# One PSUM tile of eight banks, priorities as a virtual time, an earlier load and a split last output, in a fused attention and expert kernel

## The chip, the cores and the metric

The kernel runs on one core of a Trainium2 chip. The metric is the device time of one execution in microseconds (us). TensorE (PE) multiplies matrices into PSUM, ScalarE (ACT) and VectorE (DVE) read PSUM and work on SBUF, GpSimd (POOL) works on SBUF and issues the loads, SyncE (SP) issues the stores.

## The reference

Four batches of block attention with eight heads, 768 positions and 64 channels are followed by a top-1 mixture of eight experts. A Sinkhorn iteration (five times exp, row norm, column norm) turns a small 8x8 matrix of each head into `P`, which mixes the eight blocks of keys and of values; each query block then attends to its own mixed block.

```python
for _ in range(5):
    P = np.exp(P - np.max(P, axis=-1, keepdims=True))
    P = P / (np.sum(P, axis=-1, keepdims=True) + 1e-09)
    P = P / (np.sum(P, axis=-2, keepdims=True) + 1e-09)
k_sorted = np.einsum('bhij,bhjcd->bhicd', P, k_b)
v_sorted = np.einsum('bhij,bhjcd->bhicd', P, v_b)
attn = softmax(scale * q_b @ k_sb^T)
x = (attn @ v_sb).transpose(0, 2, 1, 3).reshape(B * S, H * D)
expert_idx = np.argmax(x @ w_gate, axis=1)
out[mask] = gate_w[mask, None] * (np.maximum(xe @ w1[e], 0.0) @ w2[e])
```

## The kernel before

The four batches run as four attentions and four experts. The kernel guesses the expert of a batch from a vote over its values, loads that expert's two weight matrices alone, applies it to all 768 rows, and does rows that chose another expert only behind a branch. Work is written as tasks; a planner in Python (`Plan`) gives each task an engine, a start and PSUM banks from costs in a table, and `emit` writes the instructions in the order of those starts. Nothing is reordered later: every engine runs its instructions in that order and waits on semaphores.

The tasks of batch b, with the lines at which their instructions stand in the profile:

- loads of q, v and k (L322, L339), and of the weights w1 and w2 (L347, L350), all issued from POOL; `chain` at the end of the kernel fixes their order on POOL's queue. The weights wait for the vote.
- "vote sum", "vote pick" (PE, L547 and L556) and "vote read" (DVE, L563 and L564): the guess of the expert, which POOL reads (L570) before it issues the weight loads.
- "relay" (L586): a copy that turns v_in into vr. "q" (PE, L601), "k" (L622) and "v" (L649), each with copies out of PSUM on ACT (L307) or DVE (L309). k and v multiply with pk and pv, which are made from `P`; `P` comes from the Sinkhorn chain on ACT (L454) and DVE (L458, L460, L461).
- for each of eight steps i: scores "s" (PE, L679), "exp" (ACT, L688), values "a" (PE, L695), normalization "n" (DVE, L705 and L706), transpose "t" (PE, L714), copy "x" (L307 or L309).
- "route" (PE, L739; DVE, L747 and on): the gate weights.
- the expert, twice (two halves of the rows): eight hidden groups "h" (PE, L772) with "relu" (ACT L782 or DVE L784), then three outputs "o", each in two pieces "a" and "b" of four matmuls (PE, L777), weighed by the gate "w" (ACT L788 or DVE L790) and stored (L841).

PSUM is held as four tiles of two banks each:

```python
pairs = [psp.tile([P, 2, 512], F32, tag=f"pair{i}", name=f"pair{i}") for i in range(4)]
PAIRS = (0, 2, 4)            # s, a, later k and v: two banks at once
FFN_BANKS = (4, 5, 6, 7)     # h and o: one bank
```

A task that asks for one bank takes half of a pair tile; the bank comes free when its reader's task ends. A task's priority (`prio`) says who goes first when several could start on an engine: attention b has 10b, its route 10b+6, expert b 10b+15. `emit` also writes matmuls on an idle tile (L83, fillers) where the plan has PE waiting in the first 26 us.

The change and the steps of the prediction touch `Plan.fit`, `Plan.emit` and `Plan.schedule`, the PSUM tiles, `add_attention` (relay, priorities), `add_expert` (the cut of the last output, banks, priorities), and the order of the loads.

Of the kernel before, what the change touches and what calls it, by code (L numbers as in the profile page):

```python
# [35 lines left out]
class Plan:  # L36
# [8 lines left out]
    def __init__(self, dma_at=2.1, dma_us=2.43):  # L45
        self.tasks, self.free = [], {}
        self.bank = [0.0] * 8
        self.dma_free, self.dma_us = dma_at, dma_us
        self.order = []
# [6 lines left out]
    def fit(self, banks):  # L56
        if banks.n == 2:
            spots = [(max(self.bank[i], self.bank[i + 1]), (i, i + 1), 0) for i in range(0, 8, 2)
                     if self.bank[i] is not None and self.bank[i + 1] is not None]
        else:  # L60
            spots = []
            for i in range(8):
                if self.bank[i] is not None:
                    twin = self.bank[i ^ 1]
                    spots.append((self.bank[i], (i,), 0 if twin is None else 1))
        if banks.only is not None:
            spots = [s for s in spots if s[1][0] in banks.only]
        return spots

    def emit(self, nc, idle, pairs, warm, until):  # L70

        held, at = [0.0] * 8, warm
        for t in self.order:
            if t.engine == "pe":
                gap = t.start - at
                while gap > 0.45 and t.start < until:
                    free = [i for i in range(8) if held[i] is not None and held[i] <= at - 0.4]
                    if not free:
                        break
                    i = free[0]  # L80
                    n = min(int(gap / 0.225), 12)
                    for _ in range(n):
                        nc.tensor.matmul(out=pairs[i // 2][:, i % 2, :], lhsT=idle[:, :128],  # L83
                                         rhs=idle, start=True, stop=True)
                    at += n * 0.22
                    held[i] = at
                    gap = t.start - at - 0.2
                at = t.end
            if t.opens is not None:
                for i in t.opens.at:  # L90
                    held[i] = None
            t.run(t.engine)
            if t.closes is not None:
                for i in t.closes.at:
                    held[i] = t.end
# [16 lines left out]
    def schedule(self):  # L112
# [11 lines left out]
        while open_:  # L124
# [49 lines left out]
            if t.lands is not None:  # L174
                if t.lands:
                    self.dma_free = max(self.dma_free, end + 0.9) + t.lands * self.dma_us
                    t.end = self.dma_free + 1.6
                else:
                    t.end = end + 2.3
            if t.opens is not None:  # L180
                spots = [x for x in self.fit(t.opens) if x[0] + 0.12 <= s + 1e-9]
                if t.opens.n == 2:
                    at = min(spots, key=lambda x: (x[0], x[1]))[1]
                else:
                    at = min(spots, key=lambda x: (x[2], x[0], x[1]))[1]
                t.opens.at = at
                for i in at:
                    self.bank[i] = None
            if t.closes is not None:
                for i in t.closes.at:  # L190
                    self.bank[i] = t.end
# [12 lines left out]
def kernel(  # L204
# [19 lines left out]
    P = 128  # L224
# [19 lines left out]
    pairs = [psp.tile([P, 2, 512], F32, tag=f"pair{i}", name=f"pair{i}") for i in range(4)]  # L244

    def bank(banks, j=0):
        i = banks.at[j]
        return pairs[i // 2][:, i % 2, :]

    def both(banks):  # L250
        return pairs[banks.at[0] // 2]
# [284 lines left out]
    PAIRS = (0, 2, 4)  # L536

    def add_attention(b):
        A = 10 * b
# [11 lines left out]
        t1 = add(f"vote sum{b}", {"pe": 0.65}, run_vsum, [v_at[b], m_vm], A - 5, opens=vb)  # L551
        t2 = add(f"vote vm{b}", {"act": 0.2, "dve": 0.2}, lambda e: copy(e, vm, bank(vb)[:, :H]), [t1], A - 5, closes=vb)
# [6 lines left out]
        t3 = add(f"vote pick{b}", {"pe": 0.25}, run_pick, [t2, wv_a, wv_b], A - 5, opens=lb)  # L559
# [6 lines left out]
        t4 = add(f"vote read{b}", {"dve": 0.45}, run_read, [t3], A - 5, closes=lb)  # L566
        val = {}

        def run_w1(e):
# [3 lines left out]
        w1_at[b] = add(f"load w1.{b}", {"pool": 1.3}, run_w1, [t4, *relu_of.get(b - 2, [])], A - 4, lands=2.0)  # L573
        w2_at[b] = add(f"load w2.{b}", {"pool": 0.9}, lambda e: load_w2(val["ev"], i2),
                       outs_of.get(b - 2, []), A - 4, lands=2.0)
        top_at[b] = add(f"top{b}", {"pool": 0.2}, lambda e: nc.gpsimd.tensor_scalar(
            top[b], eids[b][:, 0:1], -1.0, float(E), op0=ALU.mult, op1=ALU.add), [t4], A)
# [4 lines left out]
        for d0 in range(0, D // 2, D // 4):  # L582
            def run_relay(e, d0=d0):
                dst = u32(vr[i2])[:, d0:d0 + D // 4, :HB, 0]
                src = u32(v_in[i2])[:, :, d0:d0 + D // 4]
# [8 lines left out]
        for g in range(3):  # L594
# [9 lines left out]
            t = add(f"q{b}.{g}", {"pe": 0.6}, run_q, [q_at[b][g], mk_ident, *scores_of.get(b - 2, [])], A + 2, opens=qb)  # L604
# [5 lines left out]
            q_ev.append(add(f"q ev{b}.{g}", evac(1024, 1.02, 1.22), run_ev, [t], A + 2, closes=qb))  # L610
# [4 lines left out]
        for g in range(3):  # L615
            kb = Banks(2, PAIRS if b else None)
# [337 lines left out]
```

## Time and profile before

| | us |
|---|---|
| median of 3 runs | 186.6 (184.68 to 187.89) |
| the profiled execution: its time | 185.21 |
| the profiled execution: its span | 183.5 |
| PE busy in the span | 155.2 |
| ACT busy | 95.7 |
| DVE busy | 83.8 |
| POOL busy | 30.3 |

The span runs from the first to the last instruction of the profiled execution; the other 1.7 us lie around it. An engine's busy time counts overlapping instructions once; PE's ends are modelled. The granted clock of TensorE is given in tenths or as a share of 2.4 GHz.

### The profile page before, as it was taken

The numbers are of one execution on the slowest core, as the hardware profiler recorded it, in microseconds if no ns is written. First come the engines' busy times: TensorE is split into PE (matmuls) and PEld (weight loads), VectorE is DVE, ScalarE is ACT, GpSimd is POOL, SyncE is SP. The second block draws the span as 40 slices with busy tenths as digits, with TensorE's granted clock in tenths as the row PEclk, the third lists the DMA queues.
The fourth block names the chain that finished last, engine by engine and source line by source line (L and its number), as shares of the span: only waits on it lengthen the run. The fifth ranks groups of instructions, "written<-read, shape, count | busy, mean of one in ns | idle before, by whom it ended". The sixth has DMA issues, their size and how long they took to land.

```text
span 183.5 us, 5246 instructions
## 1 busy us (share of the span) xinstructions
PE 155.2 (85%) x2271; PEld 96.9 (53%) x2271; DVE 83.8 (46%) x217; ACT 95.7 (52%) x159; POOL 30.3 (17%) x65
## 2 busy tenths in 40 slices
PE   7897988188989789899889799995788999998960
PEld 2365766068655465486565354772554555544520
DVE  5588687347755750087596200572765200500000
ACT  3154975119686444387665264683565454525440
POOL 7993800207500001150000001100000000000000
PEclk9999999957999999999999999999999999999995
DMA  4994599999999991999995116995001303103032
GB/s 42 214 199 69 72 198 194 215 212 153 198 180 230 242 227 32 174 237 231 210 214 142 59 57 98 197 254 91 0 4 57 116 4 114 57 15 148 8 118 64
DMA packets 13770, 24.51 MB, mean 134 GB/s; under 512 B 1328, under 2 KB 6448, under 8 KB 13744
## 3 DMA queue, kind: packets, MB, share of 16 engines
q0 software_dynamic: 9568, 17.83, 55.7%
q1 hardware_dynamic: 4032, 6.19, 9.4%
q8 instruction: 19, 0.31, 0.7%
q10 hardware_dynamic: 144, 0.13, 0.2%
q14 instruction: 7, 0.06, 0.1%
HBM read 35.68 MB, written 6.29 MB: 229 GB/s over the span
## 4 chain that ended last, share of the span: by engine, by line
PE 52%; DMA 18%; ACT 10%; DVE 9%; issue 5%; POOL 1%; POOLq 1%; DVEq 0%; ACTq 0%
PE pair L777 20%; PE pair L772 19%; DMA v_in<-in_v_dram 18%; PE pair L83 4%; ACT o L788 3%; ACT qT L307 3%; PE pair L714 2%; PE pair L649 2%; ACT ksT L307 2%; DVE vr L586 2%; ACT hT L782 2%; PE pair L695 2%; PE pair L679 1%; DVE xT L309 1%; POOL w L350 1%
## 5 line engine op out<-in xcount | busy, mean ns | idle before, releaser
L772 PE MATMUL pair<-xT,w 128*128 128x384 bf16 x256 | 47.2, 329 | 4.4 <-issue 2.1
L777 PE MATMUL pair<-w,hT 128*128 128x512 bf16 x192 | 45.5, 379 | 3.9 <-ACT o L788 2.4
L782 ACT ACTIVATE hT<-pair 128x384 bf16<-128x384 f32 x54 | 24.4, 489 | 27.0 <-PE pair L772 18.7
L772 PEld LDWEIGHTS <-w 128*128 128x128 bf16 x256 | 23.4, 98 | 17.4 <-issue 2.7
L788 ACT ACTIVATE o<-pair,gws 128x512 f32<-128x512 f32 (+1 forms) x23 | 15.4, 677 | 28.1 <-PE pair L777 15.9
L777 PEld LDWEIGHTS <-hT 128*128 128x128 bf16 x192 | 17.8, 97 | 23.1 <-issue 4.9
L688 ACT ACTIVATE ex<-pair 128x768 bf16<-128x768 f32 x32 | 25.0, 815 | 3.3 <-PE pair L679 3.2
L706 DVE TENSOR_TENSOR xo<-pair,rec 96x512 bf16<-96x512 f32 x32 | 22.0, 687 | 1.1
L83 PE MATMUL pair<-idle 128*128 128x512 bf16 x48 | 14.0, 432 | 1.8 <-DVE idle L390 1.3
L714 PE MATMUL pair<-ident,xo 96*128 96x96 bf16 x128 | 10.8, 206 | 5.5 <-DVE xT L309 2.9
L747 DVE TENSOR_REDUCE mx<-pair 128x6 f32<-128x48 f32 x4 | 0.8, 203 | 31.5 <-ACT o L788 31.5
L309 DVE COPY xT<-pair 128x384 bf16<-128x384 bf16 x23 | 8.2, 356 | 14.2 <-PE pair L777 5.4
L714 PEld LDWEIGHTS <-xo 96*128 96x128 bf16 x128 | 7.8, 97 | 11.0 <-issue 5.7
L695 PE MATMUL pair<-vs,ex 128*128 128x65 bf16 x256 | 12.9, 193 | 0.1
L695 PEld LDWEIGHTS <-ex 128*128 128x128 bf16 x256 | 10.7, 97 | 3.8 <-ACT ex L688 1.6
L649 PE MATMUL pair<-pv,vr 128*64 128x64 bf16 x512 | 10.6, 202 | 0.4 <-ACT ksT L307 0.4
L649 PEld LDWEIGHTS <-vr 128*64 128x64 bf16 x512 | 9.8, 118 | 1.3 <-issue 1.3
L679 PE MATMUL pair<-qT,ksT 64*128 64x96 bf16 x256 | 10.1, 205 | 0.4 <-ACT ksT L307 0.2
L790 DVE TENSOR_SCALAR o<-pair,gws 128x512 f32<-128x512 f32 (+1 forms) x2 | 1.2, 617 | 19.2 <-ACT o L788 18.4
L307 ACT COPY qT<-pair 128x1024 bf16<-128x1024 bf16 x9 | 8.8, 1007 | 2.0 <-PE pair L601 1.2
L679 PEld LDWEIGHTS <-ksT 64*128 64x128 bf16 x256 | 6.4, 94 | 5.9 <-issue 3.7
L307 ACT CAST vs<-pair 128x1024 bf16<-128x1024 f32 x9 | 9.2, 1029 | 0.4
(91 smaller groups left out, 150.5 us busy)
## 6 DMA issues: line engine op xcount, KB each, us to landing
w<-in_moe_w_dram POOLq DMA_DIRECT2D x8, 1024.0 KB, 10.7
out_dram<-o SPq DMA_DIRECT2D x23, 256.0 KB, 2.1
q_in<-in_q_dram POOLq DMA_DIRECT2D x4, 768.0 KB, 18.2
v_in<-in_v_dram POOLq DMA_DIRECT2D x4, 768.0 KB, 15.0
k_in<-in_k_dram POOLq DMA_DIRECT2D x3, 768.0 KB, 22.5
k_in<-in_k_dram POOLq DMA_DIRECT2D x3, 256.0 KB, 10.4
out_dram<-o ACTq DMA_DIRECT2D x1, 128.0 KB, 2.3
out_dram<-o SPq DMA_DIRECT2D x1, 128.0 KB, 2.0
```

What stands on the lines that cost most here:

```text
L83: nc.tensor.matmul(out=pairs[i // 2][:, i % 2, :], lhsT=idle[:, :128], rhs=idle, start=True, stop=True)
L307: nc.scalar.copy(dst, src)
L649: nc.tensor.matmul(out=t[f * HP:(f + 1) * HP, u, :], lhsT=vr[i2][:, d // 2, :, d % 2], rhs=pv[b][:, f * H:(f + 1) * H, :].rearrange("p h i ...
L679: nc.tensor.matmul(out=sc[:, r, h4 * BLK:(h4 + 1) * BLK], lhsT=ksT[i2][rows, x].rearrange("p f c -> p (f c)"), rhs=qT[i2][rows, x * CQ:(x ...
L688: te = add(f"exp{b}.{i}", {"act": 0.82}, lambda e, ex=ex, sbk=sbk: nc.scalar.activation(ex[:, :H * BLK].rearrange("p (t c) -> p t c", t=2) ...
L695: nc.tensor.matmul(out=av[:, h // 4, h % 4, :], lhsT=ex[:, h * BLK:h * BLK + P], rhs=vs[i2][:, h * NB + i, :D + 1], start=(h % 4 == 0), st ...
L706: nc.vector.tensor_mul(xo, av[:, :, :, :D], rec.to_broadcast([BLK, 2, 4, D]))
L714: nc.tensor.transpose(out=tp[:, dc, :], in_=xf[:, dc * P:(dc + 1) * P], identity=ident[:BLK, :BLK])
L772: nc.tensor.matmul(out=ps, lhsT=w1t[:, dc, fc * P:(fc + 1) * P], rhs=xT[:, dc, half * NH:(half + 1) * NH], start=(dc == 0), stop=(dc == DC ...
L777: nc.tensor.matmul(out=ps, lhsT=hT[:, fc, s * P:(s + 1) * P], rhs=w2t[:, fc, :], start=(fc == 0), stop=(fc == FC - 1))
L782: nc.scalar.activation(dst, src, ACT.Relu)
L788: nc.scalar.activation(dst, src, ACT.Copy, scale=gw)
```

## The change

The four pair tiles become one tile of eight banks. Of the free banks a single one is still taken beside an occupied one first and among these the one that has been free longest, now of all eight; among equals the highest number goes first. FFN_BANKS becomes None and k, v, s and a lose PAIRS, so every task may take any bank. Priorities become a virtual time: a batch has a span of 100, attention steps are 7 apart from 35 on, an expert's groups spread over the 100 after its attention, so that expert b and attention b+1 carry interleaved numbers. The relay runs on DVE alone, the first batch's in four pieces. The load of v for batch 1 moves ahead of the weights of batch 0. The PE task "swap", on which an ACT copy depends, comes after the first q transposes. `emit` counts fillers with two durations. The last output is computed as two halves of 256 columns in two banks.

```diff
     def fit(self, banks):
...
+        b, got = self.bank, []
+        for i in range(0, 8, banks.n):
+            if banks.only is not None and i not in banks.only:
+                continue
+            if banks.n == 2:
+                if b[i] is not None and b[i + 1] is not None:
+                    got.append((max(b[i], b[i + 1]), 0, i))
+            elif b[i] is not None:
+                got.append((b[i], 0 if b[i ^ 1] is None else 1, i))
+        return got
...
-                while gap > 0.45 and t.start < until:
...
+                while t.start < until and t.start - at > 0.5:
...
+                    us = 0.43 if at < warm else 0.217
+                    nc.tensor.matmul(out=psum[:, free[-1], :], lhsT=idle[:, :128], rhs=idle,
+                                     start=True, stop=True)
...
-    pairs = [psp.tile([P, 2, 512], F32, tag=f"pair{i}", name=f"pair{i}") for i in range(4)]
...
+    psum = psp.tile([P, 8, 512], F32, name="psum")
+
+    def bank(banks):
+        return psum[:, banks.at, :]
 
     def both(banks):
-        return pairs[banks.at[0] // 2]
+        return psum[:, banks.at:banks.at + 2, :]
...
-    PAIRS = (0, 2, 4)
+    SPAN, PREP, STEPS, STEP = 100, 3.5, 35, 7
...
-        for d0 in range(0, D // 2, D // 4):
+        cut = D // 4 if b else D // 8
+        for d0 in range(0, D // 2, cut):
...
-            relays.append(add(f"relay{b}.{d0}", {"dve": 0.47} if b or not d0 else {"pool": 1.2}, run_relay,
-                              [v_at[b], pads["vr", i2], *old], A - 1))
+            relays.append(add(f"relay{b}.{d0}", {"dve": 0.5 if b else 0.27}, run_relay,
+                              [v_at[b], pads["vr", i2], *old], A - 10))
...
-            sbk, ab, tb = Banks(2, PAIRS), Banks(2, PAIRS), Banks(1)
+            sbk, ab, tb = Banks(2), Banks(2), Banks(1)
...
-                     A + 4 + i * 0.1, opens=sbk)
+                     A + STEPS + i * STEP, opens=sbk)
...
-    FFN_BANKS = (4, 5, 6, 7)
+    FFN_BANKS = None
...
-                cuts = ((0, MD // 2, ("act",), "act"), (MD // 2, MD, ("dve",), "sp")) if final else (
-                    (0, MD, ("act", "dve"), "sp"),)
+                cuts = ((0, MD // 2, "act", "act"), (MD // 2, MD, "dve", "sp")) if final else ((0, MD, None, "sp"),)
                 used = []
...
+                for j, (lo, hi_, way, queue) in enumerate(cuts):
+                    pb = Banks(1, FFN_BANKS)
...
         add_attention(b)
         if b == 0:
...
+            swap_t.after.append(q_done[0][0])
...
-    chain += seq
+    seq.remove(v_at[1])
+    chain.append(v_at[1])
+    chain = chain[:5] + [v_at[1]] + seq
...
-    plan.emit(nc, idle, pairs, 2.0, 26.0)
+    plan.emit(nc, idle, psum, 1.3, 5.5, 26.0)
```

What the planner makes of this stands in the built programs. First POOL at the start. Before, from the first pv (a factor for the values of batch 0) on, it reads the vote and issues the weights w1 and w2 of batch 0, and then v, q and k of batch 1:

```order
L518 TENSOR_TENSOR pv_139<-vh,pt_v_138 128x128
L570 TENSOR_LOAD eid_129
L570 ISA x2
L347 ISA
L347 DMA w_0_96<-in_moe_w_dram 128x4x1024
L350 ISA
L350 DMA w_0_98<-in_moe_w_dram 128x8x512
L576 TENSOR_SCALAR top_133<-eid_129 128x1
L339 DMA v_in_73<-in_v_dram 128x3072
L322 DMA q_in_69<-in_q_dram 128x2x1536
L322 DMA k_in_71<-in_k_dram 128x2x1536
```

With the change, from the memsets of vs on:

```order
L386 MEMSET vs_77 48x64 x2
L330 DMA v_in_70<-in_v_dram 128x3072
L384 MEMSET vs_78 128x64
L386 MEMSET vs_78 48x64 x2
L397 IOTA rev_i 128x8
L398 CAST rev<-rev_i 128x8
L374 MEMSET vr_76 128x32x32
L377 MEMSET ksT_74 128x64x16
L436 COPY expand_v<-ident 32x384
L394 MEMSET ones 128x128
L436 COPY expand_k<-ident 32x768
L509 TENSOR_TENSOR pv_136<-vh,pt_v_135 128x128
```

The load of v for batch 1 (L330, v_in_70) has moved from behind the weights to far ahead of the vote, and POOL's copy of v_in into vr is gone from the list.

Second ACT at the start, before (sn is the Sinkhorn matrix, wv the table of the vote, qT the turned queries):

```order
L454 ACT_TABLE_LOAD
L454 ACTIVATE sn_108<-sn_108 32x64 x2
L424 CAST wv_115<-pair0_64 64x4x8 x2
L454 ACTIVATE sn_108<-sn_108 32x64 x2
L307 COPY qT0_74<-pair0_64 128x128x8
L454 ACTIVATE sn_108<-sn_108 32x64
L307 COPY qT0_74<-pair0_64 128x128x8
```

and with the change:

```order
L445 ACT_TABLE_LOAD
L445 ACTIVATE sn_105<-sn_105 32x64 x4
L298 COPY qT0_71<-psum_64 128x128x8
L415 CAST wv_112<-psum_64 64x4x8 x2
L445 ACTIVATE sn_105<-sn_105 32x64
L298 COPY qT0_71<-psum_64 128x128x8 x2
```

The two wv casts have moved from behind the second exponential to behind the fourth and the first qT copy.

Third ACT where expert 1 and attention 2 run together, before (hT is a relu, ex an exponential, o a weighed output):

```order
L307 CAST vs0_80<-pair2_66 128x64x16
L782 ACTIVATE hT2_102<-pair3_67 128x384
L307 CAST vs0_80<-pair0_64 128x64x16
L688 ACTIVATE ex0_82<-pair1_65 128x768
L782 ACTIVATE hT2_102<-pair3_67 128x384
L688 ACTIVATE ex1_83<-pair0_64 128x768
L688 ACTIVATE ex2_84<-pair2_66 128x768
L782 ACTIVATE hT2_102<-pair3_67 128x384 x2
L782 ACTIVATE hT2_102<-pair2_66 128x384
L688 ACTIVATE ex3_85<-pair0_64 128x768
```

and with the change:

```order
L298 CAST ksT0_73<-psum_64 128x64x2x8
L780 ACTIVATE o2_102<-psum_64,gws_125 128x512
L298 CAST ksT0_73<-psum_64 128x64x2x8
L780 ACTIVATE o3_103<-psum_64,gws_125 128x512
L680 ACTIVATE ex0_79<-psum_64 128x768
L780 ACTIVATE o0_100<-psum_64,gws_125 128x512
L680 ACTIVATE ex1_80<-psum_64 128x768
L774 ACTIVATE hT0_97<-psum_64 128x384
L680 ACTIVATE ex2_81<-psum_64 128x768
L680 ACTIVATE ex3_82<-psum_64 128x768
L774 ACTIVATE hT0_97<-psum_64 128x384 x3
```

The exponentials of attention 2 now stand among the outputs of expert 1's first half and the relus of its second (hT0_97); before, they stood among the relus of its first half, and the second half came with no attention beside it.

## Rows read from the trace of the kernel before

**Rows 1.** The page: busy time by engine, and the granted clock in 40 slices.

```profile
PE 155.2 (85%) x2271; PEld 96.9 (53%) x2271; DVE 83.8 (46%) x217; ACT 95.7 (52%) x159; POOL 30.3 (17%) x65
...
PEclk9999999957999999999999999999999999999995
```

**Rows 2.** Stretches: length, busy PE, PEld, DVE, ACT, POOL, clock, DMA share, GB/s.

```profile
32.87:37.50 4.63, 0.01 (x1) 0.02 (x2) 0.69 (x3) 0.49 (x1) 1.13 (x3) 0.87 1.03 209
37.50:47.00 9.50, 8.95 (x244) 7.58 (x244) 6.44 (x16) 5.69 (x8) 4.75 (x8) 0.70 1.03 180
...
47.00:178.40 131.40, 117.53 (x1538) 71.44 (x1537) 51.75 (x125) 71.47 (x122) 7.20 (x14) 1.00 0.59 127
...
13.80:20.50 6.70, 5.59 (x200) 4.55 (x200) 6.10 (x16) 3.92 (x5) 2.91 (x6) 1.00 0.28 48
```

**Rows 3.** Timeline of the start: start, us, engine, what, [idle before, releaser].

```profile
7.44 0.37 ACT L424 CAST wv<-pair 64x32 bf16<-64x32 f32 x2 [2.75 <-PE pair L416]
...
8.13 0.21 DVE L458 TENSOR_REDUCE red<-sn 32x8 f32<-32x64 f32 x1 [1.60 <-ACT sn L454]
...
10.40 0.21 DVE L461 TENSOR_TENSOR sn<-sn,red 32x64 f32<-32x64 f32 x1
...
11.72 0.25 ACT L454 ACTIVATE sn<-sn 32x64 f32<-32x64 f32 x1
...
11.92 1.51 POOL L586 COPY vr<-v_in 128x768 uint32<-128x768 uint32 x1
...
12.47 1.04 DVE L461 TENSOR_TENSOR sn<-sn,red 32x64 f32<-32x64 f32 x1
...
14.87 0.80 DVE L586 COPY vr<-v_in 128x768 uint32<-128x768 uint32 x1
...
21.29 2.22 ACT L688 ACTIVATE ex<-pair 128x768 bf16<-128x768 f32 x3
```

**Rows 4.** Timeline of PE: the wait for v of batch 1, and one kind at either clock.

```profile
37.49 0.80 PE L547 MATMUL pair<-vmask,v_in 128*128 128x8 bf16 x24 [4.62 <-DMA v_in<-in_v_dram]
...
40.35 1.92 PE L649 MATMUL pair<-pv,vr 128*64 128x64 bf16 x64
...
84.35 1.22 PE L649 MATMUL pair<-pv,vr 128*64 128x64 bf16 x64
```

**Rows 5.** Line L339, the load of v for batch 1 alone (issued at 21.0).

```profile
DMA to landing us min/median/max: 16.4/16.4/16.4
```

**Rows 6.** The page, costliest groups: count | busy us, mean ns | idle before.

```profile
L706 DVE TENSOR_TENSOR xo<-pair,rec 96x512 bf16<-96x512 f32 x32 | 22.0, 687 | 1.1
```

**Rows 7.** Waits of PE from 45 us on: us in total, times, longest.

```profile
PE pair L714 <- DVE xT L309: 2.5, 5, 0.5
PE pair L777 <- ACT o L788: 2.4, 3, 0.8
PE pair L772 <- issue: 2.1, 1, 2.1
PE pair L714 <- ACT o L788: 1.3, 3, 0.8
PE pair L772 <- DVE hT L784: 1.3, 2, 0.7
PE pair L714 <- DVE xo L706: 1.2, 3, 0.5
PE pair L777 <- ACT xT L307: 1.0, 2, 0.7
```

**Rows 8.** Timeline at 88 us: a relu on DVE, and the PE group behind it.

```profile
88.19 0.56 DVE L784 TENSOR_SCALAR hT<-pair 128x384 bf16<-128x384 f32 x1 [1.29 <-ACT hT L782]
...
88.81 0.81 PE L772 MATMUL pair<-xT,w 128*128 128x384 bf16 x4 [0.65 <-DVE hT L784]
```

**Rows 9.** Timeline of the end: the last output on ACT and DVE.

```profile
178.40 0.47 ACT L788 ACTIVATE o<-pair,gws 128x256 f32<-128x256 f32 x1 [1.16 <-PE pair L777]
...
178.90 0.48 DVE L790 TENSOR_SCALAR o<-pair,gws 128x256 f32<-128x256 f32 x1 [18.43 <-ACT o L788]
```

More of the change, by code (lines that the diff above doesn't have):

```diff
@@ L56, in fit @@
     def fit(self, banks):
[L57 to L67, printed above, removed]
@@ L73, in emit @@
+        return got
+    def emit(self, nc, idle, psum, begin, warm, until):
+        held, at = [0.0] * 8, begin
         for t in self.order:
             if t.engine == "pe":
-                gap = t.start - at
-                while gap > 0.45 and t.start < until:
-                    free = [i for i in range(8) if held[i] is not None and held[i] <= at - 0.4]
+                while t.start < until and t.start - at > 0.5:
+                    free = [i for i in range(8) if held[i] is not None and held[i] <= at - 0.3]
@@ L78, in emit @@
                     if not free:
                         break
[L80 to L87, printed above, removed]
+                    us = 0.43 if at < warm else 0.217
@@ L88, in emit @@
+                    nc.tensor.matmul(out=psum[:, free[-1], :], lhsT=idle[:, :128], rhs=idle,
+                                     start=True, stop=True)
+                    at += us
+                    held[free[-1]] = at - 0.3
                 at = t.end
             if t.opens is not None:
-                for i in t.opens.at:
-                    held[i] = None
+                for i in range(t.opens.n):
+                    held[t.opens.at + i] = None
             t.run(t.engine)
             if t.closes is not None:
-                for i in t.closes.at:
-                    held[i] = t.end
+                for i in range(t.closes.n):
+                    held[t.closes.at + i] = t.end
@@ L175, in schedule @@
                 if t.lands:
-                    self.dma_free = max(self.dma_free, end + 0.9) + t.lands * self.dma_us
+                    rate = 2.43 if self.dma_free < 13 else 2.85
+                    self.dma_free = max(self.dma_free, end + 0.9) + t.lands * rate
                     t.end = self.dma_free + 1.6
                 else:
-                    t.end = end + 2.3
+                    t.end = end + 1.8
             if t.opens is not None:
                 spots = [x for x in self.fit(t.opens) if x[0] + 0.12 <= s + 1e-9]
[L182 to L188, printed above, removed]
+                t.opens.at = min(spots, key=lambda x: (x[1], x[0], -x[2]))[2]
+                for i in range(t.opens.n):
+                    self.bank[t.opens.at + i] = None
             if t.closes is not None:
-                for i in t.closes.at:
-                    self.bank[i] = t.end
+                for i in range(t.closes.n):
+                    self.bank[t.closes.at + i] = t.end
             self.order.append(t)
@@ L550, in add_attention @@
         vm = sb([P, H], BF16, f"vm{b}")
-        t1 = add(f"vote sum{b}", {"pe": 0.65}, run_vsum, [v_at[b], m_vm], A - 5, opens=vb)
-        t2 = add(f"vote vm{b}", {"act": 0.2, "dve": 0.2}, lambda e: copy(e, vm, bank(vb)[:, :H]), [t1], A - 5, closes=vb)
+        t1 = add(f"vote sum{b}", {"pe": 0.65}, run_vsum, [v_at[b], m_vm], A - 20, opens=vb)
+        t2 = add(f"vote vm{b}", {"act": 0.2, "dve": 0.2}, lambda e: copy(e, vm, bank(vb)[:, :H]), [t1], A - 20, closes=vb)
         def run_pick(e):
@@ L557, in run_pick @@
                                  rhs=wv[:, h, :], start=(h == 0), stop=(h == H - 1))
-        t3 = add(f"vote pick{b}", {"pe": 0.25}, run_pick, [t2, wv_a, wv_b], A - 5, opens=lb)
+        t3 = add(f"vote pick{b}", {"pe": 0.25}, run_pick, [t2, wv_a, wv_b], A - 20, opens=lb)
         mx = sb([P, E], F32, f"vmx{b}")
@@ L564, in run_read @@
             nc.vector.max_index(out=eids[b], in_max=mx, in_values=bank(lb)[:, :E])
-        t4 = add(f"vote read{b}", {"dve": 0.45}, run_read, [t3], A - 5, closes=lb)
+        t4 = add(f"vote read{b}", {"dve": 0.45}, run_read, [t3], A - 20, closes=lb)
         val = {}
@@ L773, in mm_hidden, with mm_outputs @@
                              rhs=xT[:, dc, half * NH:(half + 1) * NH], start=(dc == 0), stop=(dc == DC - 1))
-    def mm_outputs(ps, w2t, hT, s, lo, hi):
+    def mm_outputs(ps, w2t, hT, s, lo, hi, d0=0, d1=MD):
         for fc in range(lo, hi):
-            nc.tensor.matmul(out=ps, lhsT=hT[:, fc, s * P:(s + 1) * P], rhs=w2t[:, fc, :],
+            nc.tensor.matmul(out=ps, lhsT=hT[:, fc, s * P:(s + 1) * P], rhs=w2t[:, fc, d0:d1],
                              start=(fc == 0), stop=(fc == FC - 1))
@@ L818, in add_expert @@
             for s in range(SUB):
-                pb = Banks(1, FFN_BANKS)
-                t1 = add(f"o{b}.{half}.{s}a", {"pe": 0.87}, lambda e, s=s, hi=hi, pb=pb: mm_outputs(
-                    bank(pb), w2s[i2], hTs[hi], s, 0, FC // 2), [w2_at[b], *relus[:FC // 2]],
-                    A + half * 0.2 + 0.1, opens=pb)
-                t2 = add(f"o{b}.{half}.{s}b", {"pe": 0.87}, lambda e, s=s, hi=hi, pb=pb: mm_outputs(
-                    bank(pb), w2s[i2], hTs[hi], s, FC // 2, FC), [t1, *relus[FC // 2:]], A + half * 0.2 + 0.1)
-                users.append(t2)
-                outs_of[b].append(t2)
                 t = half * SUB + s
```

85 lines of the change are left out of this document (44 added, 41 removed).

## The prediction

> **What bounds the kernel now.** I read the page first, then busy time by stretches, then the timelines of the stretches that lose most, then the list of waits. PE is busy 155.2 of 183.5 us [rows 1], and its granted clock dips once, in slices 9 to 11. The stretches say where it idles [rows 2]: all of 32.87 to 37.5, where DMA is at full share, and 131.40 - 117.53 = 13.9 us between 47 and 178.4, spread over many short waits. Early on it is a chain of small operations on ACT and DVE that counts [rows 3]: PE is then kept busy by fillers. The idle stretch ends with the arrival of v for batch 1 [rows 4], a load that took 16.4 us from its issue [rows 5]. In an attention DVE's largest work is the normalization [rows 6]. The many short waits are PE's waits for copies out of PSUM [rows 7, 8], and the end is two such copies in a row [rows 9]. So the bound is PE's order of work and what makes it wait, not one engine's throughput: over 47 to 178.4 ACT and DVE are busy 71.5 and 51.8 of 131.4 us.
>
> **The base.** The profiled execution took 185.21, 1.7 more than its span; the median of the runs shown is 1.4 above that. I sum against the span and add 1.7. A measurement of this kernel tells about 2% from no change.
>
> **First term, the start, up to the first softmax exponential at 21.29.** ACT's wv casts wait 2.75 us for PE, where "swap" stands behind fillers, and the third exponential of the Sinkhorn chain stands behind them: DVE idles 1.60 for it [rows 3]. In the new order the first four exponentials come ahead of the casts, so 1.60 goes. One multiplication of the chain took 1.04 instead of 0.21 while POOL ran its relay copy (1.51 from 11.92): another 0.83 goes with that copy. That is 2.4. Against it, DVE now does all relay work: two of 0.80 instead of one, +0.8. What then comes next is DVE itself, which has relays, factors and copies out of PSUM without a pause, and ACT, which still has a qT copy ahead of the fifth exponential. I take -1.2, somewhat less than 2.4 - 0.8 = 1.6. Bounds: -2.4 if the relays hide, +0.8 if the chain's gain is all lost in waits for loads.
>
> [...]
>
> **Second term, the load of v for batch 1.** It was issued at 21.0 behind both weights and landed 16.4 later, at 37.4; PE had waited 4.62 [rows 4, 5]. From 13.8 to 20.5 DMA was used to 0.28 [rows 2], because the weights wait for the vote. With the change POOL issues this load before the second vs memset, ahead of the vote. 768 KB at the 200 GB/s of the full stretches take 3.9 us, which the gap of 6.7 us holds, so neither w1 nor w2 of batch 0 comes later, and q and k of batch 1 come some 4 earlier. The 4.62 go. The clock: 0.70 over 9.50 us is 0.30 x 9.5 / 0.5 = 5.7 us at 1.2 GHz [rows 2], after PE had idled from 32.87 on; the same 64 matmuls took 1.92 there and 1.22 later [rows 4]. Half of 5.7 is 2.85. Together 7.5.
>
> What is late next: DVE in attention 0. Two relays of 0.80 for batch 1 now come ahead of its first normalization, and the vote's reading and the factors for batches 1 to 3 come between the eight normalizations (eight of 0.69 and a reciprocal each [rows 6]). From 20.1 on that is 1.6 for the relays, 8 x 0.9 for the normalizations, and some ten smaller operations (x copies, the vote's reading, factors) at half of 0.69, an estimate: 20.1 + 1.6 + 7.2 + 3.5 = 32.4, and about 33.5 with the last transposes and short waits, where PE was through at 32.87 before. So attention 0 ends 0.6 later although it begins 1.2 earlier: it grows by 1.8. PE covers part of that with the first hidden groups of expert 0. I charge 1.2. Net -6.3. Bounds: -7.5 if all is covered; -3.0 if the growth counts twice, because pv for batch 1 stands on POOL behind five load issues, and some of the clock's fall remains.
>
> **Third term, the waits from 47 on.** A pair tile has two banks, and the program waits by tile. At 88.81 PE begins a hidden group 0.65 late because DVE reads the group before it [rows 8]. These are two groups that live at the same time, so they are in the two banks of one pair, and the plan lists no such dependence: it gave out a free bank. In the built program 51 waits of PE on ACT or DVE (and 92 more among ACT, DVE and PE) are for an instruction that touches only the other bank; in the changed program, where the tile is tracked bank by bank, none. By kind [rows 7]: outputs waiting for a weighing, 2.4; hidden groups for a relu on DVE, 1.3; outputs for an x copy, 1.0; of transposes for a weighing about half of 1.3, as two of three have the other bank. That is 5.3. Transposes waiting for an x copy (2.5, five times 0.5) wait for the very bank that they reuse; with eight banks and the one longest free first I let them go: 7.8 gone. "issue" (2.1, once, in the middle of a hidden group) is no wait of the plan: it stays. New waits: an attention is now spread over the whole expert, with single groups of 0.65 to 0.87 between "n" and "t" where n takes 0.9. Transposes waited 1.2 for n, three times, up to 0.5 each [rows 7]. 24 transposes by 0.5 would be 12; I take 0.5, near the row, since other PE work lies between in the new order as well. Net -7.3. Bounds: 0 if new waits eat it all, -10.9 if of 13.9 only 3 remain. Fewer fillers (30 for 48) cost or bring nothing on their own: they fill PE where it waits.
>
> **Fourth term, the end.** ACT's half (0.47) and DVE's half (0.48) of the last output ran one after the other, being in one bank [rows 9]. With two banks ACT's falls beside the second half of PE's work: -0.5. Bounds: -0.5, and +0.5 for eight more weight loads with half-length matmuls.
>
> **Sum.** 183.5 - 1.2 - 6.3 - 7.3 - 0.5 = 168.2, and with 1.7 around it 169.9; I say 170.
>
> **Rivals.**
> - Everything goes but "issue" and about a microsecond: the third term is -10.9. 183.5 - 1.2 - 6.3 - 10.9 - 0.5 + 1.7 = 166.3. For it: ACT and DVE are half idle there, and their own waits on the other bank go too. Against it: in-order engines with finer interleaving.
> - New waits take the place of the old: the third term is 0, 177.2. For it: exponentials, relus and weighings alternate one by one on ACT in the new order, so each late one holds the next. Against it: each waits for PE work that the plan puts well ahead.
> - The clock falls in the start, since fillers are fewer and real matmuls there are small: another 5.7 us at half, +2.85, 172.8. For it: it fell after 32.87. Against it: no idle stretch of that length is left in the order.
> - Slower: the clock is given back in pieces. Place: the stretches in which an attention runs beside an expert, most of the 131 us from 47 on. If short pauses between small groups made it fall there for a third of the time, 43 us at half would cost 21.6: 170 + 21.6 = 191.6; it decides from about 31 us at half on, which cost the 15 gained. Against it: with 13.9 us of short pauses between 47 and 178.4 the clock stood at 1.00 [rows 2]. [...]
> - The change does not do what it says: the single tile is tracked as a whole. Then every wait that had one stranger's bank has seven: 5.3 would become up to 37, and 183.5 - 8.0 + 32 + 1.7 = 209. Against it: the built program's waits, as above.
>
> **Chances.** Forecast (166 to 174) 0.47; fewer waits still 0.23; new waits 0.20; clock in the start 0.05; clock in pieces 0.03; tracked as a whole 0.02. The first four are faster by over 2% (below 182.9) except for some 0.02 of the third: 0.93 faster. The last two are slower, 0.05, and 0.02 is left within 2%. The range of 8 in 10 runs from 163.5, below the second case by what the first two terms' better bounds allow (-1.2 each), to 177.
>
> **What would show it.** Right: the first softmax exponential at about 20; no PE wait of over 1 us for a load and a clock of 1.0 from 6 us to the end of PE; v for batch 1 landing near 20; waits of PE from about 40 us on that sum to 5 to 8, with no output group waiting for a weighing; one copy of 0.48 behind the last matmul. Wrong: transposes or values that wait often for n or exp, ACT without idle time beside the experts, a longer "issue", a clock below 1.0 in the middle, or an attention 0 that ends after 35.

## The result, and the profile after

The changed kernel took 169.03 us (median of 4 runs, 168.42 to 170.06); the kernel before, on the same chip, 186.0 (184.68 to 187.89). The ratio is 0.9115, 95% interval 0.9025 to 0.9204: faster by 9%. Forecast: 170.0, range 163.5 to 177. Single executions of one kernel can lie over 1.5% above its fastest; where a median below includes such ones, the median without them stands beside it. The profiled execution took 170.06 with a span of 168.4, so 15.1 less than the span before, where the sum had 15.3. The total came out; three of its four terms did not, as the stretches show.

The page of the changed kernel:

```profile
PE 152.8 (91%) x2246; PEld 95.1 (56%) x2261; DVE 84.4 (50%) x232; ACT 97.6 (58%) x147; POOL 28.6 (17%) x64
...
PEclk9999985599999999999999999999999999999999
```

PE's share rose from 85 to 91% [rows 1]. The clock still dips, earlier and for longer. Stretches of the changed kernel (columns as in [rows 2]):

```profile
13.80:20.50 6.70, 4.65 (x190) 3.93 (x190) 5.34 (x13) 3.16 (x4) 3.77 (x6) 1.00 1.07 187
24.26:34.50 10.24, 8.97 (x139) 7.25 (x140) 6.97 (x21) 4.27 (x7) 3.82 (x6) 0.50 1.16 200
37.50:47.00 9.50, 9.45 (x239) 6.48 (x235) 5.00 (x12) 6.98 (x10) 1.01 (x3) 1.00 1.16 207
47.00:163.20 116.20, 112.29 (x1500) 68.05 (x1507) 51.39 (x134) 71.67 (x108) 5.74 (x9) 1.00 0.59 131
```

From 47 us on PE now idles 116.20 - 112.29 = 3.9 us where it idled 13.9 [rows 2]: ten microseconds. DMA between 13.8 and 20.5 went from 0.28 to full share: the early load fills the pause, as planned. But 10.24 us run at half clock (0.50), with 0.320 us from one 384-column matmul to the next where it is 0.162 at 1.00; that is 1.2 and 2.4 columns a nanosecond, and at one column a clock, an estimate, the prediction's 1.2 GHz.

The other five come from 24 to 47 us. These two stretches are of the kernel before, then of the changed one:

```profile
24.00:47.00 23.00, 16.70 (x379) 13.01 (x375) 14.32 (x36) 11.95 (x19) 5.87 (x11) 0.85 1.09 194
```

```profile
24.00:47.00 23.00, 21.66 (x408) 15.65 (x409) 14.11 (x37) 13.50 (x22) 7.13 (x15) 0.78 1.15 205
```

PE's idle time there fell from 6.3 to 1.3. So 10 + 5 = 15 us of PE waits went from 24 us on; the start and the end gave nothing in this execution. The start, in the changed kernel's timeline:

```profile
12.34 0.50 DVE L452 TENSOR_TENSOR snb<-sn,red 32x64 bf16<-32x64 f32 x1
...
15.83 0.64 PE L614 MATMUL psum<-pk,k_in 128*64 128x128 bf16 x16 [0.43 <-DMA k_in<-in_k_dram]
16.30 1.14 PE L641 MATMUL psum<-pv,vr 128*64 128x64 bf16 x60
19.05 1.28 PE L641 MATMUL psum<-pv,vr 128*64 128x64 bf16 x68 [1.61 <-issue]
...
25.53 0.81 PE L538 MATMUL psum<-vmask,v_in 128*128 128x8 bf16 x24 [1.29 <-issue]
...
21.29 0.82 ACT L680 ACTIVATE ex<-psum 128x768 bf16<-128x768 f32 x1
```

The Sinkhorn chain's last multiplication starts at 12.34; in the kernel before an earlier one began at 12.47 and took 1.04 us [rows 3]. Yet the first softmax exponential is at 21.29 to the hundredth as before: PE stops for 1.61 us inside the v groups, after 60 of 128 matmuls, and nothing in the trace releases it (the profile's "issue"). A second such stop, 1.29, stands ahead of the vote's sum for batch 1. PE's waits from 45 us on, all of them:

```profile
PE psum L641 <- issue: 1.5, 1, 1.5
PE psum L706 <- DVE xo L698: 0.8, 1, 0.8
PE psum L769 <- issue: 0.6, 4, 0.2
PE psum L593 <- issue: 0.4, 1, 0.4
```

Of the kinds in [rows 7] only one wait for n is left; what remains is mostly "issue". The end:

```profile
162.31 0.47 ACT L780 ACTIVATE o<-psum,gws 128x256 f32<-128x256 f32 x1 [0.19 <-PE psum L769]
...
163.19 0.48 DVE L782 TENSOR_SCALAR o<-psum,gws 128x256 f32<-128x256 f32 x1 [13.75 <-PE psum L769]
```

ACT's half runs beside PE and one copy of 0.48 stands behind the last matmul, as forecast [rows 9].

### The profile page after: what moved, and what is told of

It is laid out like the page before. It is cut to its first block, busy times and chain, and to the rows that moved or that the text cites. A ratio compares the mean times of both kernels' runs of the same rounds, so it can differ in the third digit from the quotient of the medians.

```text
span 168.4 us, 5239 instructions
## 1 busy us (share of the span) xinstructions
PE 152.8 (91%) x2246; PEld 95.1 (56%) x2261; DVE 84.4 (50%) x232; ACT 97.6 (58%) x147; POOL 28.6 (17%) x64
## 4 chain that ended last, share of the span: by engine, by line
PE 70%; DMA 17%; issue 5%; POOL 2%; DVE 2%; ACT 1%; DVEq 0%; ACTq 0%; POOLq 0%
PE psum L764 23%; PE psum L769 22%; DMA v_in<-in_v_dram 11%; DMA k_in<-in_k_dram 7%; PE psum L687 5%; PE psum L706 4%; PE psum L671 4%; PE psum L641 4%; PE psum L614 2%; PE psum L593 2%; ACT ex L680 1%; PE psum L538 1%; PE psum L731 1%; POOL k_in L313 1%; DVE vs L300 1%
## 5 line engine op out<-in xcount | busy, mean ns | idle before, releaser
L764 PE MATMUL psum<-xT,w 128*128 128x384 bf16 x256 | 50.9, 331 | 0.0
L769 PE MATMUL psum<-w,hT 128*128 128x512 bf16 (+1 forms) x186 | 43.9, 370 | 1.2 <-issue 0.6
L780 ACT ACTIVATE o<-psum,gws 128x512 f32<-128x512 f32 (+1 forms) x24 | 16.3, 679 | 28.0 <-PE psum L769 26.4
L764 PEld LDWEIGHTS <-w 128*128 128x128 bf16 x256 | 21.7, 99 | 12.6 <-issue 0.5
L680 ACT ACTIVATE ex<-psum 128x768 bf16<-128x768 f32 x32 | 25.4, 810 | 3.4 <-PE psum L671 2.6
L774 ACT ACTIVATE hT<-psum 128x384 bf16<-128x384 f32 x42 | 20.6, 490 | 10.1 <-PE psum L764 10.0
L698 DVE TENSOR_TENSOR xo<-psum,rec 96x512 bf16<-96x512 f32 x32 | 22.0, 687 | 1.3 <-DVE rec L697 0.3
L776 DVE TENSOR_SCALAR hT<-psum 128x384 bf16<-128x384 f32 x22 | 12.3, 557 | 12.1 <-PE psum L764 11.9
L298 ACT CAST vs<-psum 128x1024 bf16<-128x1024 f32 x13 | 13.1, 1019 | 6.9 <-PE psum L641 6.1
L687 PE MATMUL psum<-vs,ex 128*128 128x65 bf16 x256 | 14.1, 201 | 0.9 <-ACT ex L680 0.9
L641 PE MATMUL psum<-pv,vr 128*64 128x64 bf16 x512 | 10.9, 198 | 3.1 <-issue 3.1
L706 PE MATMUL psum<-ident,xo 96*128 96x96 bf16 x128 | 11.6, 217 | 0.8 <-DVE xo L698 0.8
```

The source lines that it names most:

```text
L298: nc.scalar.copy(dst, src)
L641: nc.tensor.matmul(out=t[f * HP:(f + 1) * HP, u, :], lhsT=vr[i2][:, d // 2, :, d % 2], rhs=pv[b][:, f * H:(f + 1) * H, :].rearrange("p h i ...
L680: te = add(f"exp{b}.{i}", {"act": 0.82}, lambda e, ex=ex, sbk=sbk: nc.scalar.activation(ex[:, :H * BLK].rearrange("p (t c) -> p t c", t=2) ...
L687: nc.tensor.matmul(out=av[:, h // 4, h % 4, :], lhsT=ex[:, h * BLK:h * BLK + P], rhs=vs[i2][:, h * NB + i, :D + 1], start=(h % 4 == 0), st ...
L698: nc.vector.tensor_mul(xo, av[:, :, :, :D], rec.to_broadcast([BLK, 2, 4, D]))
L706: nc.tensor.transpose(out=tp[:, dc, :], in_=xf[:, dc * P:(dc + 1) * P], identity=ident[:BLK, :BLK])
```

## The experiments

Theory at this point: the tile gave most, the early load something, and the "issue" stops with the clock took part of it back. Each ratio is to the kernel before on the same chip, with its 95% interval. The edits are shown in part; "..." marks what is left out.

### The tile of eight banks, alone and undone

e1_after_pairs, the changed kernel with four pair tiles:

```
-    psum = psp.tile([P, 8, 512], F32, name="psum")
+    pairs = [psp.tile([P, 2, 512], F32, tag=f"pair{i}", name=f"pair{i}") for i in range(4)]
...
-        return psum[:, banks.at, :]
+        return pairs[banks.at // 2][:, banks.at % 2, :]
...
```

> The changed kernel, order of instructions and banks untouched, with its eight banks tracked as four tiles of two banks, as before. Theory (the waits for the other bank of a pair were worth 5.3 us and more, and the new order mixes more tasks in neighbouring banks): 174 to 178 us against 169.0 of the changed kernel, PE idle from 47 us to the end of its work 9 to 13 us instead of 4.0, with output groups and hidden groups waiting for relus, weighings and x copies again. Rival (the new order and the free choice of banks did it, the tile is a detail): 168.5 to 171 us, idle 4 to 6.

Measured: 178.05 us, ratio 0.9585 (0.9546 to 0.9624). The largest of PE's waits from 45 us on:

```profile
PE pair L769 <- ACT o L780: 2.4, 4, 0.8
PE pair L706 <- DVE xT L300: 1.6, 3, 0.5
PE pair L769 <- DVE hT L776: 1.2, 5, 0.3
PE pair L769 <- DVE xT L300: 0.9, 2, 0.4
...
PE pair L764 <- ACT hT L774: 0.8, 2, 0.4
```

e2_before_one_tile, the reverse edit in the kernel before:

> The kernel before, order and banks untouched, with one tile of eight banks tracked bank by bank. Theory: the 5.3 us of waits for the other bank go, 180 to 182 us against 186.0; transposes still wait for x copies (five times 0.5). Rival (the waits are held up by the order, and what goes at one place comes back at the next): 184.5 to 186 us.

Measured: 176.17 us (175.74 without the longest), ratio 0.9448 (0.9401 to 0.9496). Its largest waits:

```profile
PE psum L546 <- DMA v_in<-in_v_dram: 2.0, 2, 1.6
PE psum L678 <- ACT hT L781: 1.4, 1, 1.4
PE psum L648 <- issue: 1.3, 1, 1.3
PE psum L713 <- DVE xo L705: 1.1, 2, 0.8
```

The tile is worth 9.0 us in the new order and 9.5 to 9.8 in the old, with the same instructions in the same order on every engine: theory, and nearly twice its price. In the first list the kinds of [rows 7] are back: outputs behind weighings and x copies, hidden and output groups behind relus. In the second the transposes' waits for x copies (2.5) are gone too, though the banks are the old ones. PE's idle time from 47 us to its end went from 13.8 to 6.2 in the old order, and from 3.8 to 8.9 where the pairs came back.

### The early load

e3_after_v1_late moves the load back:

```
-    seq.remove(v_at[1])
-    chain.append(v_at[1])
-    chain = chain[:5] + [v_at[1]] + seq
+    chain += seq
```

> The changed kernel with the load of v for batch 1 back behind both weights of batch 0, and the order that the planner makes of it. Theory of the prediction (the load is worth 4.6 of wait and half of the clock's fall): v for batch 1 lands near 37 again and PE waits for it, 173 to 176 us against 169.0. Rival A (with the experts advancing beside the attention PE has hidden groups of expert 0 to do meanwhile): 169 to 171 us. On the stall of 1.61 us inside the v groups at 17.44 (nothing in the trace releases it): if it is PE's instruction fetch behind that load, it is gone here and the first softmax exponential starts near 20; if it belongs to the place in the program, it stays.

Measured: 171.60 us (170.85 without the longest), ratio 0.9244 (0.9176 to 0.9311). Timeline of its start:

```profile
16.69 2.44 PE L641 MATMUL psum<-pv,vr 128*64 128x64 bf16 x128
...
24.33 0.62 PE L687 MATMUL psum<-vs,ex 128*128 128x65 bf16 x8 [1.39 <-issue]
...
20.07 2.22 ACT L680 ACTIVATE ex<-psum 128x768 bf16<-128x768 f32 x3
```

The stop of 1.61 is gone and the first softmax exponential starts at 20.07, 1.22 earlier. Up to 46 us no wait of PE over 0.25 is for v of batch 1, which lands at 34.8: PE has groups of expert 0 meanwhile (rival A). The later load chain costs 2.1 at the load for batch 2. So moving the load is worth 1.8 to 2.6 us net, and the two intervals overlap; in the profiled execution it costs 1.2 of the start. How much the stop takes varies: with the load early it was 1.61 in the changed kernel and 0.56 in e4 and e12; with it late, in e3, the 128 matmuls of the v groups run without one. In e12 the first exponential came at 20.29:

```profile
18.07 1.27 PE L642 MATMUL psum<-pv,vr 128*64 128x64 bf16 x68 [0.56 <-issue]
```

e5_old_order_tile_v1 is the reverse: the kernel before with one tile, and that load in front.

> The kernel before with two parts of the change alone: one tile of eight banks, and the load of v for batch 1 ahead of the weights of batch 0. Old priorities, old restriction of banks, old relay and swap, old end. With the tile alone it took 176.2 us. Theory (the load is worth its wait of 5.1 and the second one of 1.6, and some 3 of the clock, in the old order too): 167 to 170 us, so that the new order by itself brings almost nothing over the changed kernel's 169.0. Rival (in the old order the saved wait is given back by the loads behind it and by waits for exponentials, and the new order is needed to use it): 172 to 176 us.

Measured: 174.58 us (171.46, 174.10, 175.06 and 175.12); its executions scatter too much for an interval. Against e2 the load brings 1.6 in the old order by the medians, 4.3 by the fastest execution alone, so its price there is open; the theory's 167 to 170 was not reached by any. In the profiled execution, one of 174.10, the wait of 5.1 gives way to one of 1.70 for a v copy on DVE at 21.7 and to stops without a releaser (1.79 at 43.0, 1.29 at 78.0, 1.88 at 117.8).

e12_after_old_banks puts the bank restrictions back:

```
-    FFN_BANKS = None
+    FFN_BANKS = (4, 5, 6, 7)
...
-            sbk, ab, tb = Banks(2), Banks(2), Banks(1)
+            sbk, ab, tb = Banks(2, PAIRS), Banks(2, PAIRS), Banks(1)
```

> The changed kernel with the old restriction of banks (scores, values, and the k and v groups of later batches in the first three pairs, outputs in banks 4 to 7); one tile, priorities, loads, relay and end as in the changed kernel. Two parts of the change alone (tile and load) gave 174.6 us, the whole 169.0. Theory (the priorities by virtual time bring the rest): 169 to 171 us, PE idle from 47 us to the end 4 to 6. Rival (the free choice of banks brings it): 172.5 to 175 us, with PE waiting for n and x copies.

Measured: 170.24 us (169.84 without the longest), ratio 0.9225 (0.9163 to 0.9287), with PE idle 1.8 from 47 on. The free choice of banks is worth 0.8 to 1.2 us, within the spread. What is left between e5 and e12, 4.3 by the medians and 3.1 by the fastest of each, is for the priorities, the relay, "swap", the fillers, the end and some changed costs in the planner's table (1.3 to 2.2 for the load of w1) together. That the priorities are the main part is not shown: no run takes them out alone.

### The stops without a releaser

e6_after_shift40 adds forty matmuls of 8 columns ahead of everything:

```
-                    nc.tensor.matmul(out=psum[:, free[-1], :], lhsT=idle[:, :128], rhs=idle,
...
+                    cuts = [(0, 256)] + [(256 + 8 * j, 264 + 8 * j) for j in range(4)] if at < 5.5 else [(0, 512)]
+                    for lo, hi in cuts:
+                        nc.tensor.matmul(out=psum[:, free[-1], lo:hi], lhsT=idle[:, :128], rhs=idle[:, lo:hi],
...
```

> The changed kernel with forty more tiny matmuls (8 columns) ahead of everything, in place of half of the columns of the first ten fillers; nothing else moves. Observation: in the runs so far every stall of PE over 0.3 us that nothing releases stands where 95 matmuls plus a multiple of 128 have been issued, and each ends 1.3 to 1.5 us after a 16 KB transfer of the instruction queue. Theory (PE waits for its next block of 256 instructions): the stalls move with the count, 40 matmuls earlier in the program; none in the v groups at 17.44, none ahead of the vote's sum at 24.23; instead one of 2 to 3.5 us behind the fourth matmul of the third score group, about 20 us. Rival (the stalls belong to the place in the program, or to loads that hold PE's operands): stalls of 1.6 and 1.3 us stay ahead of the same matmuls. Time: within 1.5 us of the changed kernel's by either.

Measured: 170.80 us, ratio 0.9235 (0.9144 to 0.9326), 1.8 above the changed kernel where both answers had 1.5; the clock was at half from 14.92 to 18.34 and from 25.16 to 31.99. PE's timeline:

```profile
17.57 2.54 PE L643 MATMUL psum<-pv,vr 128*64 128x64 bf16 x128
...
23.84 0.75 PE L540 MATMUL psum<-vmask,v_in 128*128 128x8 bf16 x24
...
42.21 0.53 PE L595 MATMUL psum<-ident,q_in 128*64 128x128 bf16 x5 [2.06 <-issue]
...
77.66 0.28 PE L643 MATMUL psum<-pv,vr 128*64 128x64 bf16 x6 [1.17 <-issue]
```

Both early stops left their places with 40 matmuls more ahead, so they do not belong to the place. The stop of 2 to 3.5 forecast for the third score group did not come; why is not shown. Two stops remain, 2.06 and 1.17. Counted by weight loads (one to each matmul; 15 matmul records of the changed kernel are missing), its four stops over 0.3 us without a releaser stand at 223, 351, 1246 and 1757, 93 to 95 past a multiple of 128; the one of the kernel before, 2.10 at 124.34, stands at 1886, 94 past. All five end 1.28 to 1.57 us after a 16 KB transfer of the instruction queue ended. In e4 below 128 matmuls lie between two stops, and in e9 below, with 81 matmuls more ahead, the stop in the v groups stands 47 matmuls later, which is 128 - 81. That PE waits there for instructions is the author's estimate from the count, the transfers and the shift. Why one transfer starts 0.5 us after the 95th matmul past a multiple of 128 has begun (kernel before, 18.86 to 19.39) and another 4.3 us after (changed kernel, 12.41 to 16.75) is open.

e4_after_fillers was to hold the clock:

```
+            only = None if b else (0, 2, 4)
-            sbk, ab, tb = Banks(2), Banks(2), Banks(1)
+            sbk, ab, tb = Banks(2, only), Banks(2, only), Banks(1)
...
-                while t.start < until and t.start - at > 0.5:
+                while t.start < until and t.start - at > (0.5 if at < 16.0 else 0.1):
```

> The changed kernel with the score and value groups of batch 0 kept to banks 0 to 5, so that the fillers have banks 6 and 7, and fillers for gaps of 0.1 us instead of 0.5 after 16 us: some nine fillers between 20 and 26 us where the changed kernel has none; the order of small groups there shifts a little. Theory (the clock fell at 24.26 because PE had too little to do from about 15 on): granted clock 1.00 over 24 to 34.5, attention 0 ends 2 to 4 us earlier, 165.5 to 167.5 us. Rival A (the stall of 1.61 at 17.44 alone brings the clock down, fillers behind it or not): the fall stays and the time is 168.5 to 170. Rival B (the clock holds but PE is not what limits attention 0, DVE is): clock 1.00, and only 0 to 1 us gained.

Measured: 172.81 us, ratio 0.9293 (0.9239 to 0.9347), slower than the changed kernel. PE's timeline:

```profile
18.29 1.28 PE L641 MATMUL psum<-pv,vr 128*64 128x64 bf16 x68 [0.56 <-issue]
...
25.58 0.32 PE L547 MATMUL psum<-wv,vm 128*128 128x8 bf16 x6 [3.19 <-issue]
```

The next stop, 128 matmuls on, fell into the vote and took 3.19, and the clock went to half at 24.3 as before. The theory's 1.00 did not come, and the time fits none of the three answers; none is tested cleanly, since the fillers shared the stretch with a longer stop.

### Stops and clock

e7_v1_late_shift84 and e8_v1_mid_shift84 use the edit of e6 on all 21 first fillers; e7 has the load of v late, as in e3, and e8 has it between w1 and w2 (`seq.insert(1, v_at[1])`).

> The changed kernel with the load of v for batch 1 late (171.6 us so far, with a stall of 1.39 at 22.93 and the clock at half from 24.05 for 6.8 us) and 84 more tiny matmuls in the first 21 fillers, which puts the ends of the instruction blocks into the k groups, at matmul 104 of 128 of the v groups, and past the first attention's middle. Theory of the blocks: no stall over 0.5 us between 12 and 30 us, since the fetch falls into the pause of the loads from 15.9 to 18.2. On the clock, theory A (what brings it down at 24 is the stalls of PE between 15 and 24): granted clock 1.00 from 24 to 31, and 167 to 169 us. Theory B (it is the small groups that wait for exponentials, stall or not): the clock falls as before, 170 to 171.5 us.

Measured: 168.76 us, ratio 0.9091 (0.8978 to 0.9205). The same stretch of e3, then of e7:

```profile
24.00:31.00 7.00, 6.67 (x81) 4.63 (x82) 3.90 (x9) 4.20 (x6) 0.00 (x0) 0.51 1.19 198
```

```profile
24.00:31.00 7.00, 6.61 (x112) 4.63 (x112) 6.45 (x19) 4.93 (x9) 0.00 (x0) 1.00 1.20 197
```

No stop between 12 and 40 us, a clock of 1.00 instead of 0.51, and 2.1 to 2.8 us less than e3 (the intervals overlap): as theory A has it. But the tiny matmuls also moved the rise of the clock, from 6.99 to 10.59, so the stops are not the only thing that changed. The clock fell later, at 37.9, behind a wait of 1.37 for the load.

> The changed kernel with the load of v for batch 1 between the two weights of batch 0 (behind w1, ahead of w2) and the same 84 tiny matmuls. Theory: v for batch 1 lands near 27, w2 near 32 as in the changed kernel, PE waits for neither; the start ends at 20.1 instead of 21.3 because the instruction fetch no longer stands behind that load, no stall over 0.5 before 30 us. With the clock held 164 to 166.5 us, with its fall 166.5 to 168.5. Rival (the early load is what counts, and each stall that goes comes back at another block's end): 168.5 to 171 us.

Measured: 168.62 us, ratio 0.9107 (0.9020 to 0.9194), on the border of the two. As the theory has it, the first exponential came early, at 20.33, with no stop before 30. As the rival has it, a stop of 1.91 came back at 39; v landed at 30.0 instead of 27, PE waited 1.13 for it, and the clock dipped at 30.4 and 40.7.

e9_after_split_fillers and e10_v1_mid_split_fillers shift by fillers cut in four:

```
+                    w = 128 if at < 12.0 else 512
+                    for lo in range(0, 512, w):
```

> The changed kernel, v for batch 1 early as in it; of its thirty fillers the 27 before 12 us are cut into four matmuls of 128 columns each: the same columns, 81 more matmuls, so the instruction blocks end 81 matmuls earlier in the program, nearly as in the run with 84 tiny ones that had no stall between 12 and 30 us. Theory (the stalls at 17.44 and 24.23 are block ends, and they, with few fillers, brought the clock down at 24.26): no stall over 0.5 us between 12 and 30 us, granted clock 1.00 from 8 to past 30, first softmax exponential near 20.2, and 163.5 to 166.5 us against 169.0. Rival (with that load in the queue the next block comes late wherever it ends): stalls of 1 to 3 us in the v groups or the first value groups, the clock falls, 168 to 171 us.

Measured: 169.78 us (169.59 without the longest), ratio 0.9173 (0.9132 to 0.9214): the rival. With the load early the stop came 47 matmuls later, 2.28 us behind matmul 107 of the v groups instead of matmul 60, the first exponential came at 22.86, and the clock was at half from 24.3 for 10.24 us.

> As the run with v for batch 1 between the two weights of batch 0, but with the fillers cut into four of 128 columns each instead of the 84 tiny matmuls, which had kept the clock at half until 10 us there. Theory: clock up by 7 or 8 us, first softmax exponential near 20.2 instead of 20.7, no stall before 30; the wait of 1.1 for that load at 29 and the clock's fall behind it stay: 167 to 168.5 us. Rival (the early clock is worth nothing, as the chain on DVE sets the start): 168.2 to 169.2 us, as there.

Measured: 168.89 us (168.47 without the two longest), ratio 0.9149 (0.9096 to 0.9202). The clock rose at 5.41 instead of 9.97, yet the first exponential came at 20.43, no earlier than in e8: the rival, as far as the spread lets one tell. There was no stop before 37, and the clock stayed at 1.00 until 39.5, in a stop of 2.46. In both PE idles 0.02 us from 47 on, so nothing is left to gain there but PE's own work. No version beats the changed kernel by more than the spread.

Seven profiles (the changed kernel's, e1, e3, e4, e9, e11, e12) have a stop of over 1 us between 17 and 26 us; in all seven the clock falls at 23.1 to 25.5. Of those without one, the kernel before, e2, e7, e8 and e10 keep it past 30; e5 loses it at 22.3 in its wait of 1.70, and e6 loses it at 14.9 and 25.2 with no pause over 0.5 us. In six of the seven the fall comes in a stop or about 0.1 us behind its end; in e9 it comes 2.9 us behind, and in the changed kernel the second stop had lasted 0.02 us. So the stops go with the fall, and e6 shows that it comes without them too; that they alone bring it down is not shown, since every run that lost them also moved the start of the full clock or the load.

### The relay on POOL

e11_v1_late_relay_pool is e3 with the old relay of batch 0 (`cut = D // 4`, the second half on POOL).

> The changed kernel with the load of v for batch 1 late (171.6 us; first softmax exponential at 20.07, no stall ahead of it) and the relay of batch 0 as before: halves, the second on POOL. The prediction's first term: the chain's last multiplication takes 1.0 instead of 0.65 or 0.50 and the second half of the relay is off DVE (0.8 to 0.9 less work there): first exponential at 20.0 to 20.5. Rival (the copy on POOL was the larger part of the old start): at 20.9 or later. Time 170.5 to 172.5 us by either, as the start moves by less than the spread.

Measured: 171.59 us, ratio 0.9247 (0.9180 to 0.9315). DVE, POOL and ACT in its timeline:

```profile
12.06 0.44 DVE L452 TENSOR_TENSOR snb<-sn,red 32x64 bf16<-32x64 f32 x1
...
13.78 0.99 DVE L485 TENSOR_TENSOR pk<-ksel,pt_k 128x128 bf16<-128x128 f32 x2
...
12.19 2.23 POOL L578 COPY vr<-v_in 128x768 uint32<-128x768 uint32 x1 [0.35 <-DMA v_in<-in_v_dram]
...
20.81 1.52 ACT L680 ACTIVATE ex<-psum 128x768 bf16<-128x768 f32 x2
```

The first exponential is at 20.81, between the two answers, and part of that may be a clock at half from 14.7 to 18.1: the relay's price is not settled. The last multiplication took 0.44, not the 1.0 forecast; it began 0.13 us before POOL's copy. Seen directly is that the first of the two pk products takes 0.78 beside POOL's copy (both 0.99), against 0.29 in e3 and the changed kernel without it (both 0.49).

## Why the prediction was right, and where not

- **The start: -1.2 forecast, 0 measured in the profiled execution.** The size was right: 20.07 in e3, where the load of v is late, and 20.29 in e12, where the stop is short. The step that failed is in the second term: "768 KB ... take 3.9 us, which the gap of 6.7 us holds". The gap holds the load, but in it PE stopped for 1.61, from 17.44 on, and that ate the gain. The pk products took 0.49 in the changed kernel, where POOL had done its expand copies 0.07 us earlier; in e2, where the expand_k copy ran beside it, the first of them took 0.88.
- **The load: -6.3 forecast.** The load landed at 20.4 as forecast and the wait of 4.62 went, but it was not the load's to give: with the new order it is hidden even when the load stays late (e3). Undone, it costs 1.8 to 2.6 in the new order; done alone, it brings 1.6 by the medians in the old one, with too much scatter to settle it. The failing step is "The 4.62 go", priced against the old order although the change moved that too. The half of the clock's fall, -2.85, had the wrong sign: 10.24 us at half instead of 6.83 are 1.7 more by the prediction's own pricing, an estimate. (The dip of the kernel before stands in slices 9 and 10 of [rows 1], not 9 to 11.) "No idle stretch of that length is left in the order" was true and not enough; this rival had 0.05 and came true beside the forecast. Attention 0 ended at 38.1, after the 35 named as a sign of being wrong; in e7, where the clock held and the load came late, it ended at 33.2.
- **The waits from 47 on: -7.3 forecast, -10 measured**, near the rival's -10.9. The mechanism was right (e1, e2), the price of the other bank wrong: 5.3 was PE's own waits, while the tile is worth 9.0 to 9.8. The transposes' waits for x copies (2.5), taken for waits on the very bank, went in e2 with the banks unchanged, so they too were the tile's; whether through the 92 further waits, on ACT and DVE, which the prediction counted and did not price, no run tells. The part of the 10 that is not the tile's comes with the rest of the change. New waits, +0.5, were right: 0.8, once.
- **The end: -0.5 forecast, none in the span.** The copy went: from the last matmul to the last copy's end it takes 0.57 instead of 1.07. But the last stores now follow closer: the last whole output is issued 0.67 us ahead of ACT's half instead of 1.64, and from the last copy to the last packet of the stores it takes 2.2 us instead of 1.6. That the one causes the other is not tested.
- **The sum** was right by compensation, which is luck: 1.2 and 0.5 that did not come, and a load worth less, against a tile and an order worth more.

## What to carry to other kernels

A dependency that the program has only because it tracks two buffers as one can cost more than the waits that the bounding engine shows for it (here 9.0 to 9.8 us against 5.3): price it with a kernel that changes the tracking alone. A wait seen in the old order is no price for an edit that comes together with a new order. When a load is moved into a pause of the DMA engines, look at what else used that pause: in the changed kernel a 16 KB transfer of the instruction queue ran inside the load, and PE's stop of 1.61 ended 1.34 us after that transfer.

## What the runs showed of the hardware that was not expected

PE stopped with no releaser in the trace at a fixed count: five stops of 0.38 to 2.10 us in the kernel before and the changed one, 93 to 95 past a multiple of 128 weight loads, each ending 1.28 to 1.57 us after a 16 KB transfer of the instruction queue. In the changed kernel the transfer for the stop at 17.44 ran from 16.75 to 17.71, inside the load of v, and the four stops over 0.3 us sum to 4.75 us. On the clock: from 47 us to the end of PE's work the changed kernel, with banks chosen freely, kept 1.00, and e1, with 8.9 us of short waits there, kept it too. Where the clock did fall in that stretch (e2 at 62.0, e11 at 62.5, e4 at 116.5, e5 at 121.3), a pause of 1.2 to 2.2 us stood ahead of it; e3 had a wait of 2.1 there and kept 1.00 up to 160.
